# Linear attention and a squared-ReLU MLP on one core: tile 0 loaded on two queues, measured in halves, its products put between its transposes

## The chip, the cores and the metric

The kernel runs on one core of a Trainium2 chip. The core has a matrix engine (TensorE, PE in the profile, with its weight loads shown apart as PEld), three engines for elementwise work (VectorE = DVE, ScalarE = ACT, GpSimd = POOL), SyncE (SP), which issues most loads and stores, and 16 DMA engines. The engines run side by side, each through its own queue in order, and wait for one another on semaphores. The metric is the time of the whole program on the device, in microseconds (us); lower is better.

## What is computed

A layer-normalised input goes through a linear attention with 32 heads of 16 columns and, beside it, through an MLP with a squared ReLU; both results are added to the input.

```python
# x: 2048 x 512, wqkv: 512 x 1536, wo: 512 x 512, w1: 512 x 1376, w2: 1376 x 512, all float32
xn = _layernorm(x, axis=-1)
return x + _A_ref(xn, A_wqkv, A_wo) + _B_ref(xn, B_w1, B_b1, B_w2, B_b2)
# _A_ref
q, k, v = qkv[0], qkv[1], qkv[2]                       # of x @ wqkv, by heads
phi = lambda t: jnp.where(t > 0, t + 1, jnp.exp(t)) + 1e-6
pq, pk = phi(q), phi(k)
kv = jnp.einsum("bhsd,bhse->bhde", pk, v)
z = jnp.einsum("bhsd->bhd", pk)
num = jnp.einsum("bhqd,bhde->bhqe", pq, kv)
den = jnp.einsum("bhqd,bhd->bhq", pq, z)[..., None] + 1e-6
return (num / den, heads side by side) @ wo
# _B_ref
h = xn @ w1 + b1;  r = jnp.where(h > 0, h, 0);  return (r * r) @ w2 + b2
```

## The kernel before

The 2048 rows are 16 tiles of 128 tokens. Every product in float32 is made from parts: an operand is split into a high part (a rounded copy, type fp32r) and a low part (what the rounding left), and three products, high by high, high by low and low by high, are summed in PSUM.

The work runs in stages. First, for each tile: load, mean and variance, normalisation, transposition, the projection to the keys (`pk`), phi, and the sum over the tokens of keys by tokens (`kx`). Then come small matrices per head, and after them two large passes over the tokens with queries, both MLP matrices and the output. Nothing schedules the instructions: each engine runs them in the order of the program's text (`manual_schedule`), which was written out by hand. Only the waits are put in by the framework.

The change touches the start, tiles 0 and 1 and the key weights. What happens there, by names:

- 11 matmuls on zeros (`warm`, L528) keep TensorE busy until data is there.
- `touch` (L77, L78) is a tiny load of 64 elements of `wqkv` that ScalarE issues first of all, followed by the load of its function table.
- `load_x(i, t)` (L159) has SyncE load a tile's 128 x 512 values into `xr[i]`. Behind tiles 0 and 1 stand the four chunks of the key weights (`rk`), then tiles 2 and 3.
- `measure` (L232) runs `bn_stats` and `bn_aggr` on VectorE: mean and variance in `mv`. `roots` (L244) adds 1e-5 on VectorE (for tiles 2 and 3 on GpSimd) and has GpSimd raise that to the power -0.5, into `y`.
- VectorE normalises tile 0 in two halves of 256 columns (L600) and tile 1 whole (L270), into `xp`.
- `turned_pe` (L305) has TensorE transpose the four 128 x 128 blocks of `xp[i]` into PSUM (`pt`), and then `ones(i)` (L346) has GpSimd overwrite the last column of `xp[i]` with 1. `transposed` (L314) gives back `high`, ScalarE's copy of the transposed blocks to `xs1h`, `low`, VectorE's rest in `xs1l`, and `keep_t`.
- `heads_k(j)` (L577) is ScalarE's high part of key chunk j (`wkh`), `rests_k(eng, j)` (L581) the low part (`wkl`), on GpSimd ("pool") or VectorE ("dve").
- `some(i, u, js)` (L587) are the products of tile i's chunks js (part u) with the high key part, `rest(j, i)` (L590) those of its high part with the low key part. A projection is finished by 12 such products.
- GpSimd's small copy at L611 orders the load of tiles 4 to 7 behind tile 1's normalisation.

In the order of the text, between the measuring of tiles 0 and 1 and `rest(0, 0)`:

```python
    high, low, keep0 = transposed(0, 2)
    heads_k(0)
    high()
    rests_k("pool", 0)
    some(0, 0, (0,), True)
    normalise(*two_tiles[1])
    high1, low1, keep1 = transposed(1, 2)
    heads_k(1)
```

Of the kernel before, what the change touches and what calls it, by code (L numbers as in the profile page):

```python
# [18 lines left out]
def kernel(  # L19
# [55 lines left out]
    ctx.enter_context(tc.manual_schedule())  # L75

    touch = keep.tile([D // Q * 4, 1], F32, name="touch")  # L77
    nc.scalar.dma_start(touch, wqkv.rearrange("(a b) c -> a b c", b=Q // 4)[:, 0, D:D + 1])  # L78
    nc.scalar.preload_act_table_set("natural_log_exp_and_others")

# [224 lines left out]
    def turned_pe(i, n=1):  # L305

        t = [bank(f"pt{i}{k}", "acc" if i < 2 else "ps")[:, :D // n] for k in range(n)]
        for j in range(NJ):
            k, at = divmod(j * P, D // n)
            nc.tensor.transpose(t[k][:, at:at + P], xp[i][:, j * P:(j + 1) * P], ident)  # L310
        ones(i)
        return [p.rearrange("p (j t) -> p j t", j=NJ // n) for p in t]

    def transposed(i, n=1):  # L314

        b, at = i // TB, slot(i)
        if i < NDVE:
            t = turned_pe(i, n)
# [12 lines left out]
        def keep_t():  # L331
# [5 lines left out]
            if i < NPE:  # L337
                nc.sync.dma_start(xTd[b][:, :, at], o)

        return high, low, keep_t  # L340

# [187 lines left out]
    t, rk = two("x0"), four("rk", "r0")  # L529
    for i in range(2):  # L530
        load_x(i, t[:, i:i + 1])
    def load_k(*js):
# [61 lines left out]
    two_tiles = group(0), group(1)  # L594
    for t in two_tiles:
        measure(t)
        roots(*t)
    for k in range(2):
        a = slice(k * D // 2, (k + 1) * D // 2)
        nc.vector.tensor_scalar(xp[0][:, a], xr[0][:, a], two_tiles[0][2][:, 0, 0:1], two_tiles[0][3][:, 0, :1],  # L600
                                op0=OP.subtract, op1=OP.mult)
    high, low, keep0 = transposed(0, 2)
    heads_k(0)
    high()
    rests_k("pool", 0)
    some(0, 0, (0,), True)
    normalise(*two_tiles[1])
# [3 lines left out]
    nc.gpsimd.tensor_copy(x4[:, 0, :1], xp[1][:, :1])  # L611
    load_x(4, x4)
    some(0, 0, (1,))
    low()
    some(0, 1, (0, 1))
    high(1)
# [10 lines left out]
    heads_k(2)  # L627
    rests_k("dve", 1)
    high1(1)
# [773 lines left out]
```

## Time and profile before

| | |
|---|---|
| median of 3 runs | 409.11 us (408.92 to 409.43) |
| profiled execution | 409.03 us, its span 407.3 us |
| TensorE busy | 402.2 us, 99% |
| VectorE busy | 308.0 us, 76% |
| ScalarE busy | 268.4 us, 66% |
| GpSimd busy | 49.7 us, 12% |
| moved by DMA | 49.00 MB, 120 GB/s in the mean |

The profile is of one execution. Its time is the span, from the first instruction to the last, and 1.7 us around it. A line of the timeline gives the start in us from the span's start, the length, the engine, the line of the kernel, the operation, what it writes and reads and its shape; `x4` means that four like it stand together, and the square bracket gives the idle time of the engine ahead of it and what ended that. Buffers go by the program's names, without their numbers.

### The profile page before, as it was taken

The page shows a single profiled execution, that of the slowest core. Times are in us where ns is not written, and L with a number is a line of the kernel's source. Part 1 is how long each engine was busy: PE and PEld are TensorE (multiplying, and loading weights), DVE is VectorE, ACT ScalarE, POOL GpSimd, SP SyncE. Part 2 cuts the span into 40 slices and gives each one's busy share as a digit, 9 for nine tenths or more (in the row PEclk, how much of TensorE's full clock was granted, in tenths as well). Part 3 has the DMA queues.
Part 4 walks back from the last instruction along what each step waited for, and adds up shares of the span by engine and source line. Part 5 has one row for each costly group of instructions (what it writes and reads, how often), then busy time and mean ns, then how long its engine had stood idle before and what let it go on. Part 6 is the DMA issues. An engine that isn't in the chain of part 4 may idle for free.

```text
span 407.3 us, 5632 instructions
## 1 busy us (share of the span) xinstructions
PE 402.2 (99%) x1939; PEld 331.0 (81%) x1939; DVE 308.0 (76%) x559; ACT 268.4 (66%) x466; POOL 49.7 (12%) x81
## 2 busy tenths in 40 slices
PE   8999999999999999999999999999999999999996
PEld 7888888888788888888878888888888888878885
DVE  5886666587898989988349997667989676449833
ACT  5677677556887788886818752667687856828520
POOL 5444333220000000030000300000000200001200
PEclk9999999999999999999999999999999999999999
DMA  6857646900432231380564903311222880034612
GB/s 212 278 175 224 208 163 192 256 27 0 120 90 80 77 103 27 121 200 16 217 228 146 194 19 113 106 53 52 52 80 50 226 189 26 0 108 151 105 26 103
DMA packets 46830, 49.00 MB, mean 120 GB/s; under 512 B 8337, under 2 KB 31121, under 8 KB 46546
## 3 DMA queue, kind: packets, MB, share of 16 engines
q1 hardware_dynamic: 44418, 44.46, 35.4%
q0 software_dynamic: 2304, 4.20, 6.5%
q8 instruction: 15, 0.25, 0.2%
q14 instruction: 13, 0.11, 0.1%
q10 hardware_dynamic: 80, 0.00, 0.0%
HBM read 37.76 MB, written 9.70 MB: 117 GB/s over the span
## 4 chain that ended last, share of the span: by engine, by line
PE 98%; DMA 1%; DVE 1%; ACT 0%; issue 0%
PE acc L133 37%; PE b L497 33%; PE pk L378 11%; PE kx L398 11%; PE acc L508 2%; PE pz L133 1%; DMA x<-in_A_x_dram 1%; PE b L133 1%; PE pz0b L133 1%; PE acc L515 0%; PE pt L310 0%; DVE st L236 0%; PE pkv L937 0%; PE pm L954 0%; PE end L133 0%; PE end L508 0%
## 5 line engine op out<-in xcount | busy, mean ns | idle before, releaser
L133 PE MATMUL acc<-w2r,s 128*128 128x512 f32 x477 | 112.8, 390 | 0.0
L133 PEld LDWEIGHTS acc<-w2r,s 128*128 128x128 f32 x477 | 89.4, 188 | 19.3 <-issue 0.7
L497 PE MATMUL b<-T,aop 128*128 128x512 f32 x336 | 83.5, 389 | 0.0
L497 PEld LDWEIGHTS b<-T,aop 128*128 128x128 f32 x336 | 63.0, 188 | 13.9 <-ACT t L114 0.8
L1075 POOL DMA_DIRECT2D res<-in_B_b_dram x16 | 14.4, 1067 | 276.7 <-DVE pt L438 90.4
L398 PE MATMUL kx<-pk,tok 128*128 128x512 f32 x192 | 46.0, 389 | 0.0
L398 PEld LDWEIGHTS kx<-pk,tok 128*128 128x128 f32 x192 | 36.0, 188 | 7.6 <-ACT pk L114 0.2
L497 PE MATMUL b<-xs0h,aop 128*128 128x512 f32 x112 | 36.9, 390 | 0.0
L133 PE MATMUL acc<-mh,aTsr 128*128 128x512 f32 x112 | 35.6, 389 | 0.0
L1083 DVE TENSOR_TENSOR res<-acc,res 128x512 f32<-128x512 f32 x16 | 10.7, 689 | 20.5 <-PE acc L133 19.2
L114 ACT ACTIVATE aop<-S 128x512 fp32r<-128x512 f32 x28 | 17.5, 624 | 12.5 <-DVE S L735 12.5
L359 POOL TENSOR_TENSOR tok<-xp,tok 128x512 fp32r<-128x512 f32 x15 | 20.2, 1344 | 39.6 <-ACT tok L114 39.6
L497 PEld LDWEIGHTS b<-xs0h,aop 128*128 128x128 f32 x112 | 21.0, 188 | 4.4
L133 PEld LDWEIGHTS acc<-mh,aTsr 128*128 128x128 f32 x112 | 21.0, 188 | 4.4
L125 DVE TENSOR_TENSOR w2r<-r,w2r 128x512 fp32r<-128x512 f32 (+2 forms) x35 | 23.8, 682 | 0.5 <-ACT w2r L114 0.4
L122 DVE TENSOR_TENSOR aop<-S,aop 128x512 fp32r<-128x512 f32 x28 | 19.3, 688 | 4.8 <-ACT aop L114 4.4
L122 DVE TENSOR_TENSOR s<-c,s 128x512 fp32r<-128x512 f32 x20 | 13.6, 689 | 11.4 <-ACT s L114 11.3
L497 PE MATMUL b<-xs0l,aop 128*128 128x512 f32 x56 | 21.8, 389 | 0.0
L133 PE MATMUL acc<-ml,aTsr 128*128 128x512 f32 x56 | 21.8, 389 | 0.0
L114 ACT ACTIVATE w2r<-r 128x512 fp32r<-128x512 f32 x32 | 19.6, 619 | 3.3 <-DMA out_dram<-res 2.0
L497 PE MATMUL b<-xs1h,aop 128*128 128x512 f32 x56 | 19.5, 389 | 0.0
L114 ACT ACTIVATE T<-Tf 128x512 fp32r<-128x512 f32 x16 | 9.5, 624 | 14.4 <-DVE Tf L678 14.3
(195 smaller groups left out, 751.6 us busy)
## 6 DMA issues: line engine op xcount, KB each, us to landing
r<-in_B_w_dram SPq DMA_DIRECT2D x49, 256.0 KB, 3.2
res<-in_A_x_dram SPq DMA_DIRECT2D x8, 512.0 KB, 4.2
res<-in_B_b_dram POOLq DMA_DIRECT2D x16, 256.0 KB, 5.7
out_dram<-res SPq DMA_DIRECT2D x15, 256.0 KB, 2.1
via<-xp SPq DMA_DIRECT2D x5, 512.0 KB, 2.6
xg<-via SPq DMA_DIRECT2D x20, 128.0 KB, 2.8
xTd<-t SPq DMA_DIRECT2D x8, 256.0 KB, 3.4
x<-in_A_x_dram SPq DMA_DIRECT2D x4, 512.0 KB, 4.1
```

Of the source, the lines that this page charges most:

```text
L114: nc.scalar.activation(o, i, AF.Copy, bias=bias)
L122: ENG[el].tensor_tensor(out=l, in0=src, in1=f32(h), op=OP.subtract)
L125: nc.vector.tensor_tensor(out=l, in0=src, in1=f32(h), op=OP.subtract)
L133: nc.tensor.matmul(ps, lhsT=a[u], rhs=b[v], start=first and n == 0, stop=last and n == 2)
L359: ENG[el].tensor_tensor(out=l, in0=src, in1=f32(h), op=OP.subtract)
L378: nc.tensor.matmul(ps, lhsT=cols(i)[u][:, j, slot(i)], rhs=w[v][:, j, :], start=first and n == 0, stop=last and n == len(steps) - 1)
L398: nc.tensor.matmul(kxp[c], lhsT=tok[i][:, u, c * P:(c + 1) * P], rhs=pk[i][:, v], start=i == 0 and (u, v) == first, stop=i == NT - 1 and ( ...
L497: nc.tensor.matmul(ps, lhsT=a[u][:, j * P:(j + 1) * P], rhs=b[v][:, j, :], start=first and j == 0 and n == 0, stop=last and j == 1 and n == 2,
L508: nc.tensor.matmul(ps, lhsT=s[u][:, k * P:(k + 1) * P], rhs=w2s[NF - 1][u][:, a:z], start=first and u == 0, stop=stop and u == 1)
L1075: nc.gpsimd.dma_start(r[:, i], b2[None, :].partition_broadcast(P), accum_op=OP.add)
L1083: nc.vector.tensor_tensor(out=r[:, a:z], in0=ps, in1=r[:, a:z], op=OP.add)
```

## The change

1. Tile 0 is loaded in two halves of 256 columns, the left one by SyncE's queue and the right one by ScalarE's, ahead of `touch` and the table load. Tile 1 stays on SyncE's queue.
2. `bn_stats` of tile 0 runs on each half, and `bn_aggr` joins the two. VectorE's order is then: tile 1's `bn_stats`, tile 0's left half normalised, tile 1's `bn_aggr` and addition, tile 0's right half normalised.
3. `turned_pe` no longer issues the transposes itself but gives back `part(k)`, and `transposed` takes a function `between` that it calls after the first part. For tile 0 that is the first key chunk's high part, the left half's high part and the first product.
4. The left half's low part and its product come ahead of tile 1.
5. The low part of key chunk 1 is made on GpSimd, behind the copy of L611, instead of on VectorE.

```diff
-    touch = keep.tile([D // Q * 4, 1], F32, name="touch")
-    nc.scalar.dma_start(touch, wqkv.rearrange("(a b) c -> a b c", b=Q // 4)[:, 0, D:D + 1])
-    nc.scalar.preload_act_table_set("natural_log_exp_and_others")
...
     def turned_pe(i, n=1):
         t = [bank(f"pt{i}{k}", "acc" if i < 2 else "ps")[:, :D // n] for k in range(n)]
-        for j in range(NJ):
-            k, at = divmod(j * P, D // n)
-            nc.tensor.transpose(t[k][:, at:at + P], xp[i][:, j * P:(j + 1) * P], ident)
-        ones(i)
-        return [p.rearrange("p (j t) -> p j t", j=NJ // n) for p in t]
-
-    def transposed(i, n=1):
+
+        def part(k):
+            for at in range(0, D // n, P):
+                nc.tensor.transpose(t[k][:, at:at + P], xp[i][:, k * D // n + at:][:, :P], ident)
+            if k == n - 1:
+                ones(i)
+
+        return [p.rearrange("p (j t) -> p j t", j=NJ // n) for p in t], part
+
+    def transposed(i, n=1, between=None):
...
+        if i < NDVE:
+            for k in range(n):
+                part(k)
+                if between and k == 0:
+                    between(high, low)
         return high, low, keep_t
...
     t, rk = two("x0"), four("rk", "r0")
-    for i in range(2):
-        load_x(i, t[:, i:i + 1])
+    touch = keep.tile([D // Q * 4, 1], F32, name="touch")
+    left, right = slice(0, D // 2), slice(D // 2, D)
+    xr[0] = t[:, 0]
+    nc.sync.dma_start(xr[0][:, left], xf[:P, left])
+    nc.scalar.dma_start(xr[0][:, right], xf[:P, right])
+    nc.scalar.dma_start(touch, wqkv.rearrange("(a b) c -> a b c", b=Q // 4)[:, 0, D:D + 1])
+    nc.scalar.preload_act_table_set("natural_log_exp_and_others")
+    load_x(1, t[:, 1:])
...
     two_tiles = group(0), group(1)
-    for t in two_tiles:
-        measure(t)
-        roots(*t)
-    for k in range(2):
-        a = slice(k * D // 2, (k + 1) * D // 2)
-        nc.vector.tensor_scalar(xp[0][:, a], xr[0][:, a], two_tiles[0][2][:, 0, 0:1], two_tiles[0][3][:, 0, :1],
-                                op0=OP.subtract, op1=OP.mult)
-    high, low, keep0 = transposed(0, 2)
-    heads_k(0)
-    high()
+    _, st, mv, y = two_tiles[0]
+    for k, a in enumerate((left, right)):
+        nc.vector.bn_stats(st[:, k, :], xr[0][:, a])
+    nc.vector.bn_aggr(mv[:, 0, :], st[:, :2, :])
+    roots(*two_tiles[0])
+
+    def half(a):
+        nc.vector.tensor_scalar(xp[0][:, a], xr[0][:, a], mv[:, 0, 0:1], y[:, 0, :1], op0=OP.subtract, op1=OP.mult)
+
+    nc.vector.bn_stats(two_tiles[1][1][:, 0, :], xr[1])
+    half(left)
+    nc.vector.bn_aggr(two_tiles[1][2][:, 0, :], two_tiles[1][1][:, 0, :])
+    roots(*two_tiles[1])
+    half(right)
+
+    def between(high, low):
+        heads_k(0)
+        high()
+        some(0, 0, (0,), True)
+
+    high, low, keep0 = transposed(0, 2, between)
     rests_k("pool", 0)
-    some(0, 0, (0,), True)
+    low()
+    some(0, 1, (0,))
     normalise(*two_tiles[1])
     high1, low1, keep1 = transposed(1, 2)
     heads_k(1)
     nc.gpsimd.tensor_copy(x4[:, 0, :1], xp[1][:, :1])
     load_x(4, x4)
+    rests_k("pool", 1)
     some(0, 0, (1,))
-    low()
-    some(0, 1, (0, 1))
+    some(0, 1, (1,))
...
-    rests_k("dve", 1)
```

TensorE's queue at the start, before: `pt_159` and `pt_160` are the two halves of tile 0, `pt_171` and `pt_172` those of tile 1, `pk_140` is tile 0's projection.

```order
L528 MATMUL warm<-const-float32-0.0 128x128 x11
L310 MATMUL pt_159<-ident,xp_80 128x128 x2
L310 MATMUL pt_160<-ident,xp_80 128x128 x2
L378 MATMUL pk_140<-wkh,xs1h 128x512
L310 MATMUL pt_171<-ident,xp_80 128x128 x2
L310 MATMUL pt_172<-ident,xp_80 128x128 x2
L378 MATMUL pk_140<-wkh,xs1h 128x512
L378 MATMUL pk_140<-wkh,xs1l 128x512 x2
L378 MATMUL pk_140<-wkl,xs1h 128x512
```

TensorE's queue at the same place in the changed kernel, where the halves of tile 0 are `pt_161` and `pt_162`, those of tile 1 `pt_175` and `pt_176`, and tile 0's projection is `pk_141`.

```order
L532 MATMUL warm<-const-float32-0.0 128x128 x11
L307 MATMUL pt_161<-ident,xp_77 128x128 x2
L382 MATMUL pk_141<-wkh,xs1h 128x512
L307 MATMUL pt_162<-ident,xp_77 128x128 x2
L382 MATMUL pk_141<-wkh,xs1l 128x512
L307 MATMUL pt_175<-ident,xp_77 128x128 x2
L307 MATMUL pt_176<-ident,xp_77 128x128 x2
L382 MATMUL pk_141<-wkh,xs1h 128x512
L382 MATMUL pk_141<-wkh,xs1l 128x512
L382 MATMUL pk_141<-wkl,xs1h 128x512
```

The first product now stands between tile 0's halves, the second between tile 0 and tile 1; four products stand ahead of the first one with the low key part (`wkl`), as before.

GpSimd's queue from the two powers on, before: the `MEMSET`s are `ones(0)` and `ones(1)`, `wkl` is the low part of key chunk 0, and `y_197` belongs to tile 2.

```order
L248 TENSOR_TENSOR y_145<-y_145,power 128x1
L248 TENSOR_TENSOR y_148<-y_148,power 128x1
L348 MEMSET xp_80 128x1
L583 TENSOR_TENSOR wkl<-rk,wkh 128x512
L348 MEMSET xp_80 128x1
L611 COPY x_134<-xp_80 128x1
L247 TENSOR_SCALAR y_197<-mv_196 128x1
L248 TENSOR_TENSOR y_197<-y_197,power 128x1
```

GpSimd's queue in the changed kernel, where the second `wkl` is that of key chunk 1 and `y_200` belongs to tile 2.

```order
L244 TENSOR_TENSOR y_146<-y_146,power 128x1
L244 TENSOR_TENSOR y_149<-y_149,power 128x1
L352 MEMSET xp_77 128x1
L593 TENSOR_TENSOR wkl<-rk,wkh 128x512
L352 MEMSET xp_77 128x1
L633 COPY x_135<-xp_77 128x1
L593 TENSOR_TENSOR wkl<-rk,wkh 128x512
L243 TENSOR_SCALAR y_200<-mv_199 128x1
L244 TENSOR_TENSOR y_200<-y_200,power 128x1
```

The order up to the first `wkl` is the same; its memset still stands behind all of tile 0's transposes. The second `wkl` is new ahead of tile 2's steps.

VectorE's queue at the start, before: `x_112` holds tiles 0 and 1, the third and sixth rows are the additions of 1e-5 for tiles 0 and 1.

```order
L236 BN_STATS st_143<-x_112 128x6
L237 BN_AGGR mv_144<-st_143 128x2
L247 TENSOR_SCALAR y_145<-mv_144 128x1
L236 BN_STATS st_146<-x_112 128x6
L237 BN_AGGR mv_147<-st_146 128x2
L247 TENSOR_SCALAR y_148<-mv_147 128x1
L600 TENSOR_SCALAR xp_80<-x_112,mv_144,y_145 128x256 x2
L270 TENSOR_SCALAR xp_80<-x_112,mv_147,y_148 128x512
L329 TENSOR_TENSOR xs1l<-pt_159,xs1h 128x2x128
L329 TENSOR_TENSOR xs1l<-pt_160,xs1h 128x2x128
```

VectorE's queue in the changed kernel, with the same roles for `x_109`, `y_146` and `y_149`.

```order
L607 BN_STATS st_144<-x_109 128x6 x2
L608 BN_AGGR mv_145<-st_144 128x2
L243 TENSOR_SCALAR y_146<-mv_145 128x1
L614 BN_STATS st_147<-x_109 128x6
L612 TENSOR_SCALAR xp_77<-x_109,mv_145,y_146 128x256
L616 BN_AGGR mv_148<-st_147 128x2
L243 TENSOR_SCALAR y_149<-mv_148 128x1
L612 TENSOR_SCALAR xp_77<-x_109,mv_145,y_146 128x256
L328 TENSOR_TENSOR xs1l<-pt_161,xs1h 128x2x128
L266 TENSOR_SCALAR xp_77<-x_109,mv_148,y_149 128x512
L328 TENSOR_TENSOR xs1l<-pt_162,xs1h 128x2x128
```

Tile 0's left half now stands ahead of tile 1's `bn_aggr` and addition, and its low part (`xs1l`) ahead of tile 1's normalisation.

More of the change, by code (lines that the diff above doesn't have):

```diff
@@ L307, in turned_pe @@
         t = [bank(f"pt{i}{k}", "acc" if i < 2 else "ps")[:, :D // n] for k in range(n)]
-        for j in range(NJ):
-            k, at = divmod(j * P, D // n)
-            nc.tensor.transpose(t[k][:, at:at + P], xp[i][:, j * P:(j + 1) * P], ident)
-        ones(i)
-        return [p.rearrange("p (j t) -> p j t", j=NJ // n) for p in t]
-    def transposed(i, n=1):
+        def part(k):
[5 more added lines that the diff above has]
+    def transposed(i, n=1, between=None):
         b, at = i // TB, slot(i)
         if i < NDVE:
-            t = turned_pe(i, n)
+            t, part = turned_pe(i, n)
         else:
```

## The prediction

> **What bounds the kernel now.** I read the page first, for the engine that is always busy and for its clock.
>
> ```profile
> span 407.3 us, 5632 instructions
> PE 402.2 (99%) x1939; PEld 331.0 (81%) x1939; DVE 308.0 (76%) x559; ACT 268.4 (66%) x466; POOL 49.7 (12%) x81
> PEclk9999999999999999999999999999999999999999
> PE 98%; DMA 1%; DVE 1%; ACT 0%; issue 0%
> ```
>
> TensorE is busy for 99% of the span, and the chain that ended last is 98% TensorE. So the change can act only through the moment at which TensorE's unbroken run begins, or through holes that it opens in that run. The chain in order of time (start, length, what) and the list of all that TensorE waited for show where the run begins:
>
> ```profile
> 0.79 2.85 DMA x<-in_A_x_dram
> ...
> 3.66 0.70 DVE st L236
> ...
> 6.14 0.45 PE pt L310 x2
> ...
> 7.99 4.38 PE pk L378 x19
> ...
> 12.81 3.71 PE pk L378 x16
> 16.51 5.47 PE kx L398 x24
> 21.98 2.72 PE pk L378 x12
> ```
> ```profile
> PE pt L310 <- DVE xp L600: 0.7, 1, 0.7
> ```
>
> The load of tile 0 lands at 0.79 + 2.85 = 3.64. From 7.99 on TensorE works without a hole: 19 products in 4.38 us, 0.23 us each, and 12 in 2.72 later. Apart from its start its only listed wait is the 0.7 us for tile 0's normalised half. What the change is worth is therefore read in the first 13 us, and a shift there is carried to the end whole. The timeline of that stretch (start, length, engine, line, operation; idle time before it and its releaser in brackets) carries the terms below:
>
> ```profile
> 0.83 4.57 PE L528 MATMUL warm<-const-float32-0.0 128*128 128x128 f32 x22 [0.83 <-PEq L1389]
> ...
> 4.61 0.15 DVE L247 TENSOR_SCALAR y<-mv 128x1 f32<-128x1 f32 x1
> ...
> 4.92 0.57 POOL L248 TENSOR_TENSOR y<-y,power 128x1 f32<-128x1 f32 x1 [1.76 <-DVE y L247]
> 5.24 0.63 ACT L114 ACTIVATE wkh<-rk 128x512 fp32r<-128x512 f32 x1 [2.58 <-DMA rk<-in_A_wqkv_dram]
> ...
> 5.61 0.15 DVE L247 TENSOR_SCALAR y<-mv 128x1 f32<-128x1 f32 x1
> 5.68 0.73 DVE L600 TENSOR_SCALAR xp<-x,mv,y 128x256 f32<-128x256 f32 x2
> ...
> 6.14 0.76 PE L310 MATMUL pt<-ident,xp 128*128 128x128 f32 x4 [0.74 <-DVE xp L600]
> 6.54 0.55 DVE L270 TENSOR_SCALAR xp<-x,mv,y 128x512 f32<-128x512 f32 x1
> 6.62 0.39 ACT L326 ACTIVATE xs1h<-pt 128x256 fp32r<-128x256 f32 x1 [0.75 <-PE pt L310]
> ...
> 6.97 0.16 POOL L348 MEMSET xp<- 128x1 f32 x1 [0.46 <-PE pt L310]
> ...
> 7.05 0.50 PE L378 MATMUL pk<-wkh,xs1h 128*128 128x512 f32 x1
> 7.06 1.30 POOL L583 TENSOR_TENSOR wkl<-rk,wkh 128x512 fp32r<-128x512 f32 x1
> ...
> 7.39 0.60 PE L310 MATMUL pt<-ident,xp 128*128 128x128 f32 x4
> ...
> 7.83 0.82 DVE L329 TENSOR_TENSOR xs1l<-pt,xs1h 128x256 fp32r<-128x256 f32 x2 [0.37 <-ACT xs1h L326]
> ...
> 8.41 0.19 PEld L378 LDWEIGHTS pk<-wkl,xs1h 128*128 128x128 f32 x1 [0.16 <-POOL xp L348]
> 8.53 0.39 PE L378 MATMUL pk<-wkl,xs1h 128*128 128x512 f32 x1
> ...
> 8.67 0.70 DVE L236 BATCH_NORM_STATS2 st<-x 128x6 f32<-128x512 f32 x1
> ...
> 9.50 0.66 DVE L583 TENSOR_TENSOR wkl<-rk,wkh 128x512 fp32r<-128x512 f32 x1
> 9.68 0.58 POOL L247 TENSOR_SCALAR y<-mv 128x1 f32<-128x1 f32 x1 [1.16 <-DVE mv L237]
> 10.34 0.57 POOL L248 TENSOR_TENSOR y<-y,power 128x1 f32<-128x1 f32 x1
> ...
> 11.23 0.52 DVE L270 TENSOR_SCALAR xp<-x,mv,y 128x512 f32<-128x512 f32 x1
> ...
> 12.21 0.60 PE L310 MATMUL pt<-ident,xp 128*128 128x128 f32 x4
> ```
>
> Two things stand out. VectorE starts tile 0's first half only at 5.68, although GpSimd's power is done at 4.92 + 0.57 = 5.49, because tile 1's statistics (last small step at 5.61) are queued ahead of it. And GpSimd's low part of the first key chunk ends at 7.06 + 1.30 = 8.36, just before TensorE asks for it at 8.41: that product is the fifth of the projection, and it has no slack to give.
>
> **The change part by part.** *The load.* Both halves together are the same bytes as before. The halves' landing is not in the trace; the nearest rows are those of DMAs by size (KB each, median us to landing), and the traffic at that time (busy time of each engine, clock, DMA share, GB/s).
>
> ```profile
> r<-in_B_w_dram SPq DMA_DIRECT2D x49, 256.0 KB, 3.2
> ...
> r<-in_B_w_dram SPq DMA_DIRECT2D x5, 128.0 KB, 2.6
> ...
> touch<-in_A_wqkv_dram ACTq DMA_DIRECT2D x1, 0.2 KB, 3.0
> ```
> ```profile
> 3.00:4.00 1.00, 1.00 (x7) 1.00 (x7) 0.34 (x1) 0.00 (x0) 0.16 (x1) 1.00 1.06 365
> ```
>
> Early bound: 128 KB lands 0.6 us sooner than 256 KB, so 3.64 - 0.6 = 3.04. Late bound: ScalarE's own queue landed even 0.2 KB only at 0.79 + 3.0 = 3.79, and 128 KB at 365 GB/s are 0.36 us, together 4.15. I take 3.64 for the later half, between the two: the same bytes through engines that are fully used (share 1.06) should end at the same time; and the left half at least 0.35 us sooner. The Trainium skill, "DMA: Bandwidth & Descriptors", section "Issuing engines are not separate DMA queues", speaks against a gain here: DMAs from several engines share the same 16 DMA engines, and only the issue time is saved. No run here shows yet whether it holds for this pair; by it the sum stands as taken, and by the early bound it would be 0.4 us better.
>
> *The statistics.* Rows by shape, with mean ns, give what halving the width does on VectorE:
>
> ```profile
> L329 DVE TENSOR_TENSOR xs1l<-pt,xs1h 128x256 fp32r<-128x256 f32 x4 | 1.7, 423 | 0.4 <-ACT xs1h L326 0.4
> ...
> L329 DVE TENSOR_TENSOR xs1l<-pt,xs1h 128x512 fp32r<-128x512 f32 x1 | 0.7, 693 | 0.1
> ```
>
> So after the right half lands I expect 0.42 us instead of 0.69 (between 0.35, half, and 0.69, no gain): the small step that was at 4.61 comes at 4.34. GpSimd starts 0.31 us after that (4.92 - 4.61) and takes 0.57, to 5.22; with 0.05 for the signal VectorE's left half starts at 5.27 instead of 5.68, a gain of 0.41. Tile 1's statistics pass, now ahead of it, runs from 4.41 to 5.10 and is hidden under GpSimd's power, as long as tile 1 has landed by 4.6. Before, its last small step at 5.61 with a pass of 0.70 ahead puts that landing at 4.9 at the latest; at 4.9 the left half would come at 5.6 and 0.33 of the gain would be lost. Transposes follow 0.46 later (6.14 - 5.68), at 5.73; the warm-up ends at 0.83 + 4.57 = 5.40 and doesn't bind. ScalarE's copy follows 0.48 after that (6.62 - 6.14), at 6.21, clear of its key-chunk copy (5.24 to 5.87), and the first product 0.43 later, at 6.64 instead of 7.05. Up to here it is 0.41 us faster.
>
> *The order.* The right half's two transposes now stand behind that product. Behind it the next TensorE step can start after 0.23 us (the pitch above) to 0.34 (7.05 to 7.39): 6.87. Two transposes take 0.38 to the end of the last (0.11 of pitch, from four in 0.60, and 0.27): 7.25, where before tile 0's transposes ended at 6.14 + 0.76 = 6.90. GpSimd's queue waits for just this: its memset of the last column overwrites what the transposes read, and the low part of chunk 0 stands behind it. Before it started 0.16 after the end of the transposes (7.06 - 6.90); so now at 7.41, ends at 8.71, and the product that needs it starts 0.17 later (8.53 - 8.36), at 8.88. Four products are done ahead of it in both orders, so this is a loss of 0.35 us for everything behind. With the upper bounds (0.34 and 0.45 for the transposes' start and length, the last from the chain's 6.14 row) it is 0.53. I take 0.45.
>
> TensorE alone would not be late: tile 1's normalisation on VectorE now stands behind the low part of tile 0's left half, so 6.60 + 0.03 + 0.40 (pitch of 7.83's two) = 7.03, plus 0.55 makes 7.58; tile 1's transposes follow at 7.63, and the fifth product could start at 8.5, as before. The hole that opens, 0.35 to 0.5 us, is GpSimd's. The Trainium skill, "SBUF — State Buffer", section "Who interferes with whom", says that GpSimd and certain VectorE steps lock each other out of a shared port for a whole instruction. The rows of 6.54 and 7.06 overlap by 0.03 us, which is within what GpSimd's spans can show; by the rule the low part could not start before 7.58, and the loss would be 0.52, inside the bounds above.
>
> *The second low part.* VectorE loses 0.66 us at 9.50; GpSimd gains 1.30 ahead of tile 2's small steps. Its chunk 0 ends at 8.8, chunk 1 with the memset and the small copy before it at 9.0 to 10.3; TensorE needs it about nine products after the fifth, at 11.0. Tile 2's two steps follow to 11.5 (0.58 and 0.57), its normalisation ends at 12.1, and its transposes stand at 12.21 + 0.45 = 12.66. So it is covered by 0.5 us; without the cover it would cost the rest. The freed VectorE time is on no wait that ends last.
>
> *What else moves.* The touch and the table load start one DMA issue later; the first key chunk is wanted by ScalarE at 5.24 and could come 0.3 us later without harm. The load of tile 2 is now issued only when the right half has landed, and is read at 8.67, 5 us after that. All cost nothing.
>
> Sum: the profiled execution took 409.03 us, of which 407.3 are the span and 1.73 lie around it. 409.03 + 0.45 = 409.48, and from the median of the runs, 409.11, it is 409.56. I predict **409.5 us**.
>
> **The rivals.** *A, the forecast*: TensorE's fifth product waits for GpSimd; +0.2 to +0.7 us with a landing between 3.5 and 3.8. For it: the row 8.41 and its releaser. Chance 0.53.
>
> *B, the halves land early* (3.04 to 3.4): the left half would be normalised at 4.7, then the warm-up's end and the key-chunk copy at 5.87 bind; the first product comes at about 6.2, the fifth at 8.43 instead of 8.53. That is -0.1 to +0.1 us, 409.0 to 409.2. For it are the 128 KB rows, against it the full DMA engines. Chance 0.22.
>
> *C, slower: ScalarE's queue lands late*. The measuring of tile 0 ends with the later of two queues; at 4.15 all of the above is 0.51 later, +1.0 us, 410.1. It turns from A where the landing passes about 4.0. For it is the touch row, against it that this tiny DMA shared its engines with tile 0's load. Chance 0.19.
>
> *D, the clock*: the warm-up's pitch of 4.57 / 22 = 0.21 us against 0.11 for the same shape in 7.39's row shows a half-speed TensorE at first. More idle time between 5.4 and 9 us could bring that back: 4 us of work at half speed lose some 2 us, 411. The Trainium skill, "TensorE: Matmul & The Clock Gate", Part 1, gives about 3.4 us of idling for that; no hole here would be longer than 0.8 us. Against it also: before had 0.74 us idle at the same place and no drop shows in its clock row. Chance 0.03.
>
> *E, a gain from something that the rows don't show*: 0.03.
>
> **How the numbers follow.** A measurement of this kernel tells about 0.2%, 0.8 us, from no change. The range takes A and B whole and C up to its price, with the 0.1 us by which runs lie off their median: 409.0 to 410.2. Only D and E lie outside, and the tails of A and C. Faster by over 0.2% needs E: 0.04 with a little of B. Slower by over 0.2% needs D or most of C: 0.19. The rest, 0.77, is within 0.2%.
>
> **What would show it.** In the profile after: tile 0's statistics step at 4.3; the first product at about 6.6; chunk 0's low part on GpSimd starting at 7.4 and not before the last transpose of tile 0; a TensorE hole of 0.3 to 0.5 us with GpSimd as its releaser ahead of the first product with the low key part; tile 2's transposes at 12.6. I am wrong if GpSimd starts that low part at 7.06 or sooner, if the hole is not there, or if the right half lands outside 3.5 to 3.8.

## The result, and the profile after

| | before | after |
|---|---|---|
| median of 13 runs each, side by side | 409.09 us (408.59 to 411.27) | 410.14 us (409.73 to 411.41) |
| ratio after / before, 95% interval | | 1.0024 [1.0013, 1.0036] |
| profiled execution | 409.03 us, span 407.3 | 410.27 us, span 408.6 |

The change makes the kernel 1.05 us slower. The bound of 0.2% lies inside the interval. In the one execution of the kernel after above 411 us TensorE's clock dropped for a while (granted clock 0.996 over the whole span); the last section comes back to this, and it doesn't set the median.

The page of the kernel after: TensorE is as busy as before, 403.3 us instead of 402.2, and the chain that ended last is TensorE's for 97%.

```profile
span 408.6 us, 5635 instructions
PE 403.3 (99%) x1939; PEld 331.5 (81%) x1939; DVE 307.4 (75%) x559; ACT 268.2 (66%) x466; POOL 50.1 (12%) x82
PE 97%; issue 1%; DMA 1%; DVE 1%; POOL 0%; POOLq 0%
```

The list of what TensorE waited for in the kernel after (us in total, times, longest) has two entries that before did not have, one for ScalarE's copy of tile 0's left half, one for GpSimd:

```profile
PE pk L382 <- ACT xs1h L325: 0.9, 1, 0.9
...
PE pk L382 <- POOL xp L352: 0.2, 1, 0.2
```

The chain that ended last, in order of time, shows that TensorE's unbroken run begins at 9.48 with the fifth product (before has no hole from its first product, at 7.05, on, and its fifth is at 8.53), and that the first big step behind the projection of tile 1 (`kx`) comes at 17.59 instead of 16.51:

```profile
0.79 2.42 DMA x<-in_A_x_dram
...
9.48 3.93 PE pk L382 x16
...
17.59 5.45 PE kx L402 x24
```

These 1.08 us, of the 1.24 between the two profiled executions, are carried to the end. The timeline of the first 10 us of the kernel after has where they arise:

```profile
0.83 5.03 PE L532 MATMUL warm<-const-float32-0.0 128*128 128x128 f32 x22 [0.83 <-PEq L1410]
...
3.23 0.75 DVE L607 BATCH_NORM_STATS2 st<-x 128x6 f32<-128x256 f32 x2 [3.23 <-DMA x<-in_A_x_dram]
...
5.18 0.41 DVE L612 TENSOR_SCALAR xp<-x,mv,y 128x256 f32<-128x256 f32 x1 [0.16 <-POOL y L244]
5.66 0.68 PE L307 MATMUL pt<-ident,xp 128*128 128x128 f32 x2
6.30 0.63 ACT L110 ACTIVATE wkh<-rk 128x512 fp32r<-128x512 f32 x1 [3.23 <-DMA rk<-in_A_wqkv_dram]
6.83 0.37 ACT L325 ACTIVATE xs1h<-pt 128x256 fp32r<-128x256 f32 x1
7.25 0.51 PE L382 MATMUL pk<-wkh,xs1h 128*128 128x512 f32 x1 [0.92 <-ACT xs1h L325]
7.57 0.54 DVE L266 TENSOR_SCALAR xp<-x,mv,y 128x512 f32<-128x512 f32 x1
7.60 0.38 PE L307 MATMUL pt<-ident,xp 128*128 128x128 f32 x2
8.04 0.11 POOL L352 MEMSET xp<- 128x1 f32 x1 [1.42 <-PE pt L307]
8.13 1.29 POOL L593 TENSOR_TENSOR wkl<-rk,wkh 128x512 fp32r<-128x512 f32 x1
...
8.17 0.66 PE L307 MATMUL pt<-ident,xp 128*128 128x128 f32 x4
...
8.89 0.40 PE L382 MATMUL pk<-wkh,xs1l 128*128 128x512 f32 x1
...
9.48 0.50 PE L382 MATMUL pk<-wkl,xs1h 128*128 128x512 f32 x1 [0.18 <-POOL xp L352]
```

Read it in two pieces. Up to tile 0's first transposes everything is early: 5.66 instead of 6.14. Then ScalarE gets the first key chunk only at 6.30 (before: 5.24), its copy of the left half is queued behind that, and the first product starts at 7.25, 0.20 later than before's 7.05. In the second piece, from the first product to the fifth (the first one with `wkl`), 2.23 us pass (7.25 to 9.48), where before needed 1.48 (7.05 to 8.53): the 0.75 us between them are the chain right half's transposes (7.60 to 7.98), memset (8.04), low part (8.13 to 9.42), product (9.48). 0.20 and 0.75 make the 0.95 by which the fifth product is late.

Not all of the 0.75 is GpSimd's. The product ahead of the fifth starts at 8.89, and products follow one another every 0.23 us, so TensorE alone would have reached the fifth at about 9.12, 1.87 us behind the first. That is 0.39 more than the 1.48 of before, because tile 1's normalisation stands behind the left half's low part now and tile 1's transposes come only at 8.17. GpSimd's chain, which runs beside this one and ends later, adds 0.36.

The DMA issues of the first 10 us (count, KB each, median us to landing): the halves landed sooner than tile 0's 256 KB did (2.85 in before), and only 0.2 us apart.

```profile
x<-in_A_x_dram ACTq DMA_DIRECT2D x1, 128.0 KB, 2.6
x<-in_A_x_dram SPq DMA_DIRECT2D x1, 128.0 KB, 2.4
touch<-in_A_wqkv_dram ACTq DMA_DIRECT2D x1, 0.2 KB, 3.7
```

### The profile page after: what moved, and what is told of

Its sections match the earlier page's. It is cut to its first block, busy times and chain, and to the rows that moved or that the text cites. A ratio compares the mean times of both kernels' runs of the same rounds, so it can differ in the third digit from the quotient of the medians.

```text
span 408.6 us, 5635 instructions
## 1 busy us (share of the span) xinstructions
PE 403.3 (99%) x1939; PEld 331.5 (81%) x1939; DVE 307.4 (75%) x559; ACT 268.2 (66%) x466; POOL 50.1 (12%) x82
## 4 chain that ended last, share of the span: by engine, by line
PE 97%; issue 1%; DMA 1%; DVE 1%; POOL 0%; POOLq 0%
PE acc L129 37%; PE b L501 33%; PE kx L402 11%; PE pk L382 11%; PE acc L512 2%; PE pz L129 1%; PE b L129 1%; PE pz0b L129 1%; DMA x<-in_A_x_dram 1%; PE acc L519 0%; PE pkv L958 0%; PE pm L975 0%; POOL y L244 0%; DVE st L607 0%; PE end L129 0%
## 5 line engine op out<-in xcount | busy, mean ns | idle before, releaser
L1104 DVE TENSOR_TENSOR res<-acc,res 128x512 f32<-128x512 f32 x16 | 10.7, 689 | 20.7 <-PE acc L129 19.3
```

Source lines behind the costliest of these rows:

```text
L1104: nc.vector.tensor_tensor(out=r[:, a:z], in0=ps, in1=r[:, a:z], op=OP.add)
```

## The experiments

The table has, for each kernel, the median, the median of before in the same job, the ratio with its interval, and from its profile's timeline: the start of tile 0's first statistics (tile 0 is there), of ScalarE's high part of key chunk 0, of the first product, of the fifth, and the time between these two. All times in us.

| kernel | median (runs) | before | ratio | tile 0 | chunk 0 | first | fifth | between |
|---|---|---|---|---|---|---|---|---|
| before | 409.09 (13) | | | 3.66 | 5.24 | 7.05 | 8.53 | 1.48 |
| after | 410.14 (13) | 409.09 | 1.0024 [1.0013, 1.0036] | 3.23 | 6.30 | 7.25 | 9.48 | 2.23 |
| e1 touch first | 412.49 (6) | 409.10 | 1.0080 [1.0067, 1.0094] | 5.84 | 6.00 | 8.96 | 11.85 | 2.89 |
| e2 no touch | 409.41 (11) | 409.10 | 1.0005 [0.9996, 1.0013] | 3.52 | 5.01 | 7.14 | 8.61 | 1.47 |
| e3 memset behind | 410.24 (10) | 409.10 | 1.0030 [1.0021, 1.0039] | 3.68 | 5.14 | 7.01 | 9.64 | 2.63 |
| e4 both | 412.90 (6) | 409.10 | 1.0096 [1.0080, 1.0112] | 5.08 | 5.71 | 8.09 | 11.35 | 3.26 |
| e5 after again | 411.37 (1) | | | 3.25 | 6.45 | 7.40 | 10.56 | 3.16 |
| e6 load only | 409.56 (11) | 409.13 | 1.0009 [1.0001, 1.0018] | 3.52 | 5.43 | 6.84 | 8.73 | 1.89 |
| e7 order only | 409.70 (11) | 409.13 | 1.0008 [0.9994, 1.0021] | 3.31 | 5.14 | 6.70 | 8.92 | 2.22 |
| e8 normalise first | 411.69 (6) | 409.13 | 1.0073 [1.0053, 1.0094] | 3.57 | 5.78 | 7.15 | 10.13 | 2.98 |
| e9 GpSimd only | 409.04 (11) | 408.98 | 1.0000 [0.9992, 1.0009] | 3.68 | 6.02 | 7.07 | 8.54 | 1.47 |
| e10 after, no touch | 410.16 (6) | 408.98 | 1.0032 [1.0020, 1.0043] | 3.66 | 5.63 | 7.22 | 9.43 | 2.21 |
| e11 load, old order | 409.28 (11) | 408.98 | 1.0006 [0.9997, 1.0015] | 3.62 | 5.14 | 7.10 | 8.58 | 1.48 |

For e1 and e4 "tile 0" is the later half. In the profiles of e1, e4 and e5 TensorE's clock was halved for a while ahead of the fifth product. Letters in the expectations name theories. The first four runs set T against O. T: `touch`, now behind the right half on ScalarE's queue, makes the key chunk late, and that is the loss. O: the loss is GpSimd's, whose memset stands behind the last transposes of tile 0.

### e1, after with the touch issued first

```diff
+    nc.scalar.dma_start(touch, ...)
     nc.scalar.dma_start(xr[0][:, right], xf[:P, right])
-    nc.scalar.dma_start(touch, ...)
```

> The changed kernel with one edit: ScalarE issues the small touch of the weights first and tile 0's right half second. Theory T (the touch opens the way for the weight loads, and 0.44 us of delay on it made the first key chunk 1.06 us late): ScalarE's first key chunk starts at 5.2 to 5.4 again instead of 6.30, the first product comes at 6.6 to 6.8 instead of 7.25, the first product with the low key part at 8.8 to 9.0 instead of 9.48, and the time is +0.3 to +0.6 us over before. Rival Q (two queues share the DMA engines and slow the weights, whatever the touch does): the key chunk stays at 6.1 to 6.4 and the time at +0.9 to +1.2 us.

Measured: 412.49, 2.35 above the kernel after. Five of the six executions had a granted clock of 0.996 or less over the span; the sixth took 411.19, 1.05 above the kernel after. T fell: the key chunk came at 6.00, not at 5.24, although the touch was first. What the edit did do was to make the right half late. The timeline and the DMA issues of this kernel:

```profile
3.06 0.43 DVE L607 BATCH_NORM_STATS2 st<-x 128x6 f32<-128x256 f32 x1 [3.06 <-DMA x<-in_A_x_dram]
5.84 0.43 DVE L607 BATCH_NORM_STATS2 st<-x 128x6 f32<-128x256 f32 x1 [2.35 <-DMA x<-in_A_x_dram]
7.93 0.56 PE L307 MATMUL pt<-ident,xp 128*128 128x128 f32 x2 [2.57 <-DVE xp L612]
```
```profile
x<-in_A_x_dram ACTq DMA_DIRECT2D x1, 128.0 KB, 4.4
```

The same 128 KB on the same queue took 2.6 us as that queue's first DMA and 4.4 behind a DMA of 0.2 KB. It was also issued later, at 1.38 instead of 0.79, and so behind the 256 KB of tile 1 (1.24); whether the tiny DMA or that place made it late is not shown. That a half on ScalarE's queue lands late is rival C, which the change itself avoids by issuing the half first.

### e2, before without the touch

```diff
-    nc.scalar.dma_start(touch, ...)
```

> The kernel before without the touch of the weights (64 values that nothing reads). Theory T: without it the first key chunk comes 0.8 us or more later than its 5.24, the first product at 7.25 instead of 7.05, and the time rises by 0.2 to 0.8 us. Rival Q: the chunk stays at 5.1 to 5.3 and the time is the same within 0.1 us.

Measured: 409.41, a difference from before that the interval doesn't tell from none. The first product is at 7.14 and the fifth at 8.61, where before has 7.05 and 8.53. The touch is no help to the key chunk and no harm, so T has nothing left here; e10 takes the touch out of the kernel after.

### e3, after with the memset of tile 0 behind the low part

```diff
-            if k == n - 1:
+            if k == n - 1 and i:
                 ones(i)
...
     rests_k("pool", 0)
+    ones(0)
```

> The changed kernel with one edit: GpSimd makes the first key chunk's low part ahead of its memset of tile 0's last column, so that it no longer waits for tile 0's transposes. Theory O (the order on GpSimd opened the hole ahead of the first product with the low key part): the low part starts when the high part is done, 7.0 instead of 8.13, that product comes at 9.1 instead of 9.48, and the time is +0.6 to +0.8 us over before. Rival P (TensorE's own order makes it late, GpSimd only looked like it): the product stays at 9.4 to 9.5 and the time at +1.0 us.

Measured: 410.24, no better than after. Yet O's mechanism is there, as the timeline shows: with the memset out of the way GpSimd starts the low part at 7.04, before the right half's transposes and not after them. The gain is eaten by VectorE's normalisation of tile 1, which takes 1.30 us instead of 0.54:

```profile
7.04 1.27 POOL L593 TENSOR_TENSOR wkl<-rk,wkh 128x512 fp32r<-128x512 f32 x1
7.33 1.30 DVE L266 TENSOR_SCALAR xp<-x,mv,y 128x512 f32<-128x512 f32 x1
8.69 0.66 PE L307 MATMUL pt<-ident,xp 128*128 128x128 f32 x4 [0.72 <-DVE xp L266]
9.64 0.40 PE L382 MATMUL pk<-wkl,xs1h 128*128 128x512 f32 x1
```

The normalisation is issued at 7.33, within GpSimd's instruction, and ends only behind it; tile 1's transposes then wait 0.72 us. The Trainium skill, "SBUF — State Buffer", section "Who interferes with whom", says that GpSimd and a VectorE step such as `tensor_scalar` in its two-port form exclude each other for a whole instruction, and that the one issued first wins. This trace agrees: the normalisation ends 0.32 us behind the low part, at 8.63 and 8.31, and in e8 below by the same 0.32, at 8.52 and 8.20. So the memset's late place keeps the low part out of the normalisation's way; taking it away trades one wait of TensorE for another. No kernel here shows O without that collision. Nor could O have won back all of the 0.75: TensorE's own order, 1.87 us from the first product to the fifth, would have put the fifth at about 8.88 here, an estimate from the rows of the kernel after.

### e4, e1 and e3 together

```diff
 # e1, and e3
-    nc.scalar.dma_start(touch, ...)          # behind the right half
+    nc.scalar.dma_start(touch, ...)          # ahead of it
     rests_k("pool", 0)
+    ones(0)
```

> The changed kernel with both edits, the touch first and the low part ahead of the memset. If T and O are the two causes, the first product comes at 6.6 to 6.8, the first with the low key part at 8.5 to 8.7, and the time is within 0.2 us of before. If only one of them holds, it is the time of that one alone: +0.4 (T) or +0.7 (O).

Measured: 412.90. The right half came at 5.08, the normalisation of tile 1 took 1.30 us again. Both effects are there at once, and neither edit helps. Five of the six executions had a dropped clock, as in e1.

### e5, the kernel after once more

> The changed kernel once more, unaltered, for a second profile of it. Its first profile had ScalarE's first key chunk at 6.30, while the run with the memset moved, whose loads are the same, had it at 5.14. Theory V (the landing of the first loads changes from execution to execution, and the order alone costs about 1 us): the chunk comes at another time than 6.30 by more than 0.3 us, and the first product with the low key part still at 9.2 to 9.6, 0.7 to 1.0 us later than before. Rival L (late weights are the rule with the right half on ScalarE's queue): 6.1 to 6.5 again.

Measured: one execution of 411.37 us at a clock of 0.996. Tile 0 came at 3.25 and the key chunk at 6.45, as in the first profile of this kernel (3.23 and 6.30). So what L says came again, but L is no rule: with the right half first on ScalarE's queue the chunk came at 5.14 in e3 and, below, at 5.43 (e6), 5.78 (e8), 5.63 (e10) and 5.14 (e11). In addition the clock dropped from 7.30 to 10.7, which is taken up at the end.

### e6 and e7, the two parts of the change by themselves

e6 is the kernel before with the halved load, its statistics and VectorE's new order up to the normalisation of tile 0; TensorE's and GpSimd's order and the rest stay. e7 is the kernel before with the first product between the transposes and the left half's low part ahead of tile 1; load and statistics stay. Both leave key chunk 1's low part on VectorE.

```diff
 # e6
-    for i in range(2):
-        load_x(i, t[:, i:i + 1])
+    nc.sync.dma_start(xr[0][:, left], xf[:P, left])
+    nc.scalar.dma_start(xr[0][:, right], xf[:P, right])
+    load_x(1, t[:, 1:])
 ...
+    nc.vector.bn_stats(two_tiles[1][1][:, 0, :], xr[1])
+    half(left)
+    nc.vector.bn_aggr(two_tiles[1][2][:, 0, :], two_tiles[1][1][:, 0, :])
+    roots(*two_tiles[1])
+    half(right)
 # e7
-    high, low, keep0 = transposed(0, 2)
+    high, low, keep0 = transposed(0, 2, between)
     rests_k("pool", 0)
+    low()
+    some(0, 1, (0,))
```

> The kernel before with the loading and the measuring of the changed one alone: two queues, halves, VectorE's new order, and all of tile 0's transposes together again, ahead of the first product; the second low part back on VectorE. Theory V: the first product with the low key part comes at 8.1 to 8.4 and the time is 0.1 to 0.4 us below before. Rival L: the late weights cost 0.3 to 0.8 us here too.

> The kernel before with the order of the products alone: the first product between tile 0's halves, the low part of the left half ahead of tile 1's normalisation; loads, statistics and the second low part as before. Theory V: the low key part starts on GpSimd at 7.8 to 8.0 instead of 7.06, its product comes at 9.2 to 9.5, and the time is +0.7 to +1.0 us. Rival L: within 0.3 us of before.

Measured: 409.56 for e6, 409.70 for e7, 0.43 and 0.57 above before. e7's interval includes a ratio of 1, and before had three executions of 410 us or more in that job; but the lowest of e7's eleven, 409.57, lies above 19 of before's 23. With e9's 0.06 the three parts add to 1.06 us, near the change's 1.05. This is no proof that the parts are the change's: what costs e6 its time, as shown below, is not found in the kernel after. e7's loss is less than expected (0.7 to 1.0), with GpSimd at 7.58 and the fifth product at 8.92, both sooner than expected. Its timeline has the forecast chain:

```profile
6.70 0.50 PE L386 MATMUL pk<-wkh,xs1h 128*128 128x512 f32 x1 [0.47 <-ACT xs1h L329]
7.48 0.12 POOL L356 MEMSET xp<- 128x1 f32 x1 [1.33 <-PE pt L311]
7.58 1.29 POOL L591 TENSOR_TENSOR wkl<-rk,wkh 128x512 fp32r<-128x512 f32 x1
8.92 0.51 PE L386 MATMUL pk<-wkl,xs1h 128*128 128x512 f32 x1 [0.16 <-POOL xp L356]
```

Tile 0 happened to come at 3.31 in this execution, 0.35 earlier than in before's. Even so the fifth product is 0.39 later; from the first product on it takes 2.22 us, as in the kernel after.

e6 is neither V's gain nor L's loss by late weights: its chunk, at 5.43, was in time for a copy at 6.41. The timeline tells why the fifth product is late, though the first is 0.21 earlier than before's:

```profile
6.24 0.66 POOL L244 TENSOR_TENSOR y<-y,power 128x1 f32<-128x1 f32 x1 [0.81 <-DVE y L243]
6.93 0.55 DVE L266 TENSOR_SCALAR xp<-x,mv,y 128x512 f32<-128x512 f32 x1 [0.46 <-POOL y L244]
7.13 1.50 POOL L585 TENSOR_TENSOR wkl<-rk,wkh 128x512 fp32r<-128x512 f32 x1
7.53 0.66 PE L306 MATMUL pt<-ident,xp 128*128 128x128 f32 x4 [0.20 <-DVE xp L266]
8.73 0.45 PE L374 MATMUL pk<-wkl,xs1h 128*128 128x512 f32 x1
```

With tile 0's left half ahead of tile 1's aggregation, tile 1's power comes later on GpSimd, so its normalisation starts at 6.93 instead of 6.54. It now begins ahead of GpSimd's low part and holds that one up, 1.50 us instead of 1.30: the lock of e3 with the roles exchanged. The low part ends at 8.63, 0.27 later than before's 8.36. That is just covered: TensorE has no idle time from tile 1's transposes on, and these, at 7.53 instead of 7.39, carry the late normalisation to the fifth product. The chain that ended last goes through them and not through GpSimd.

### e8, after with the low part first and tile 1's normalisation ahead of the left half's low part

```diff
 # e3, and
     ones(0)
+    normalise(*two_tiles[1])
     low()
     some(0, 1, (0,))
-    normalise(*two_tiles[1])
```

> The changed kernel with GpSimd's first low key part ahead of the memset, and tile 1's normalisation on VectorE ahead of the low part of tile 0's left half, so that neither the transposes nor the normalisation stand behind the other. Theory K (with only the memset moved, GpSimd's 1.3 us low part kept VectorE's normalisation of tile 1 waiting, 1.30 us instead of 0.54): the normalisation takes 0.55 again, tile 1's transposes start at 7.5 to 7.9, the product with the low part at 8.4 to 8.8, and the time is within 0.3 us of before. Rival: the normalisation is long for another reason and stays at 1.3 us, +0.8 us.

Measured: 411.69. This median lies between three executions of 410.83 to 410.97 and three of 412.41 to 413.64 with a dropped clock (0.996 or less); already the first three are about 0.7 us above the kernel after. K's cause is there, but the edit is no remedy: the normalisation took 1.53 us, not 0.55. In the timeline GpSimd's low part starts 0.06 us ahead of the normalisation and keeps it out all the same, and the left half's low part is then late too:

```profile
6.93 1.27 POOL L593 TENSOR_TENSOR wkl<-rk,wkh 128x512 fp32r<-128x512 f32 x1
6.99 1.53 DVE L266 TENSOR_SCALAR xp<-x,mv,y 128x512 f32<-128x512 f32 x1 [0.46 <-POOL y L244]
8.90 0.50 PE L382 MATMUL pk<-wkh,xs1l 128*128 128x512 f32 x1 [1.03 <-DVE xs1l L328]
```

### e9, before with the second low part on GpSimd

```diff
     load_x(4, x4)
+    rests_k("pool", 1)
...
-    rests_k("dve", 1)
```

> The kernel before with the second key chunk's low part alone moved to GpSimd. Forecast from the cover seen in the profiles (0.3 to 0.5 us ahead of tile 2's normalisation): tile 2's transposes at 12.1 to 12.4 as before (12.21), the time within 0.15 us of before. Rival: its 1.3 us on GpSimd push tile 2's power and normalisation, transposes at 12.5 or later, +0.3 us or more.

Measured: 409.04 against 408.98, ratio 1.0000, with tile 2's transposes at 12.18 (before 12.21): the second low part is covered. Its profile has something else. The key chunk came at 6.02, on the old load with one queue, and the copy of tile 0 was still in time:

```profile
6.02 0.63 ACT L114 ACTIVATE wkh<-rk 128x512 fp32r<-128x512 f32 x1 [3.37 <-DMA rk<-in_A_wqkv_dram]
...
6.63 0.38 ACT L326 ACTIVATE xs1h<-pt 128x256 fp32r<-128x256 f32 x1
7.07 0.50 PE L378 MATMUL pk<-wkh,xs1h 128*128 128x512 f32 x1
```

So a late chunk is not peculiar to the two queues, and here it had just no cost: the copy started 0.47 behind the transposes (6.16), where before has 0.48. In the kernel after and in e5, where the copy did wait for the chunk's, it started 0.53 behind that one (6.30 and 6.83, 6.45 and 6.98). So for a copy at 6.21, as the prediction had it, the chunk must come by 5.68.

### e10, after without the touch

```diff
-    nc.scalar.dma_start(touch, ...)
```

> The changed kernel without the touch of the weights (64 values that nothing reads). With two queues the first key chunk came at 5.14 to 6.45 in seven profiles, with one at 5.01 to 5.24 in three. Theory W (the touch, now behind the right half, falls into the loads and holds the weights up): the chunk comes at 5.0 to 5.3, the first product at 6.6 to 6.9, the time 0.3 to 0.6 us below the changed kernel's 410.1. Rival Z (two queues on the same engines hold them up): still 5.6 or later, the time within 0.2 us of the changed kernel's.

The theories here were W, that the late key chunk is what costs the kernel after its gain, so that it runs faster when the chunk is in time; and Z, that the order sets the time whichever of the two loads is early. Measured: 410.16, as the kernel after. The timeline:

```profile
3.66 0.75 DVE L606 BATCH_NORM_STATS2 st<-x 128x6 f32<-128x256 f32 x2 [3.66 <-DMA x<-in_A_x_dram]
5.63 0.63 ACT L110 ACTIVATE wkh<-rk 128x512 fp32r<-128x512 f32 x1 [3.12 <-DMA rk<-in_A_wqkv_dram]
6.07 0.67 PE L307 MATMUL pt<-ident,xp 128*128 128x128 f32 x2 [0.21 <-DVE xp L611]
7.22 0.50 PE L382 MATMUL pk<-wkh,xs1h 128*128 128x512 f32 x1 [0.47 <-ACT xs1h L325]
9.43 0.50 PE L382 MATMUL pk<-wkl,xs1h 128*128 128x512 f32 x1 [0.17 <-POOL xp L352]
```

The chunk was in time, and the first product is at 7.22 nevertheless: now tile 0 came at 3.66, as in before, and the two transposes took 0.67 us, where e6's took 0.44. W fell as the only reason. Z held: 2.21 us from the first product to the fifth, and the same time in the end.

### e11, e6 with VectorE's old order

```diff
     nc.vector.bn_stats(two_tiles[1][1][:, 0, :], xr[1])
-    half(left)
     nc.vector.bn_aggr(two_tiles[1][2][:, 0, :], two_tiles[1][1][:, 0, :])
     roots(*two_tiles[1])
+    half(left)
     half(right)
```

> The run with the loading and measuring alone, with VectorE's old order: tile 1's aggregate and addition ahead of tile 0's halves. Theory Y (with the new order GpSimd gets tile 1's power 0.4 us later, tile 1's normalisation came at 6.93 instead of 6.54, and that ate what the halves brought): the normalisation at 6.3 to 6.6, tile 1's transposes at 7.1 to 7.4, the time 0.2 to 0.5 us below that run's 409.56, so 409.1 to 409.35. Rival: late weights cost it, whatever VectorE's order; 409.5 to 409.7.

Theory Y was that e6's loss comes from VectorE's new order and not from the two queues. Measured: 409.28, not to be told from before. The normalisation of tile 1 is back at 6.59, and the fifth product at 8.58: in the profile Y held. In time it is not shown. e11 is 0.28 below e6, but in another job; each against before in its own job they are 0.30 and 0.43 above it, and the intervals overlap. The run also says that the halved load and statistics, put into the old order, bring nothing that can be measured. None of the eleven is faster than the kernel before.

## Why the prediction was right, and where a step failed

The direction, the place and the mechanism were right. The time lies in the range, but 0.64 us above the 409.5 forecast, because one term of the sum did not arrive. That 410.14 is in the range is partly luck: the range reached to 410.2 for the price of C, and C did not happen.

*The order: right in its mechanism.* From the first product to the fifth the prediction had 2.24 us (6.64 to 8.88); the kernel after has 2.23, e10 2.21, e7 2.22. That it agrees so well is luck, since two errors cancel. The right half's transposes began 0.35 behind the product (0.34 in e10 and e7), at the upper bound and not at the 0.23 of the sum. And the fifth product began 0.06 behind the end of the low part (0.06 in e10, 0.05 in e7), not 0.17: that was read from before, where the fifth product has no idle time ahead of it and so did not wait for GpSimd. GpSimd's start 0.16 after the last transposes became 0.15 (7.98 to 8.13), its length 1.29. Tile 1's normalisation also ended just ahead of that start, at 8.11; but in e6 the low part starts while that normalisation runs and is only longer for it, so the start is the memset's. e3 shows that without the memset GpSimd does start earlier. What the prediction did not see is that this would not help: the memset hid a collision with tile 1's normalisation.

That "TensorE alone would not be late" held only together with the gain of the load. The prediction's 7.58 was the end of tile 1's normalisation, and 7.57 is where it started; it ended at 8.11, as the copy ahead of it all was 0.62 late. Counted from the first product the forecast for TensorE's own order was good, 1.86 us (8.5 - 6.64) and 1.87 measured, but that is 0.39 more than before's 1.48. GpSimd's own addition of 0.36 lies in the forecast 0.35 to 0.5; the profile shows only 0.18 us of it as idle time, as the product ahead (0.40 long, at a pitch of 0.23) fills the rest.

*The load: the failed step.* The 0.41 us by which the first product was to come sooner never came; it was 0.20 later in the kernel after. The term needed the left half to land at least 0.35 us ahead of the right one, so that only one statistics step of 0.42 us would follow the last landing. In all seven profiles in which ScalarE issued the right half first, the halves landed 0.1 to 0.2 us apart, and the two steps took 0.75 us from the first landing on, where the whole tile's one step took 0.69. From the start of the statistics to the first product before needs 3.39 us; e3 and e6, with the chunk in time and transposes of 0.44, need 3.33 and 3.32, e11 with VectorE's old order 3.48. So the new order of VectorE brings about 0.15 us, the halves take some 0.08 of it back, and the term is 0.06 or 0.07 instead of 0.41.

That the transposes still came at 5.66 in the kernel after, where 5.73 was forecast, is luck: tile 0 was there at 3.23, 0.43 sooner than in before (the right half at about 3.4, 0.79 + 2.6, outside the 3.5 to 3.8 of the prediction). In e10, with 3.66, they came at 6.07. Then two things took that gain and 0.20 more. First, the prediction put down that the key chunk "could come 0.3 us later without harm"; it came 1.06 later. Had ScalarE been free when the transposes ended at 6.34, its copy would have stood at about 6.37 and not at 6.83: 0.46 us. Second, the two transposes took 0.68 us instead of 0.44: 0.24 us. Without both the first product would have been at 7.25 - 0.46 - 0.24 = 6.55, near the 6.64 forecast, with the early landing in it. This last sum is argued from one profile, not shown by a run. The sum after that step: instead of -0.41 + 0.76 it is +0.20 + 0.75.

*A cost at nothing that isn't.* VectorE's new order was costed as a pure gain. By itself it delays tile 1's normalisation by 0.39 us (e6, 6.93 instead of 6.54) and with it the fifth product; what that costs in time is not clear of the noise (e6 and e11). In the kernel after it lies under the left half's low part, which the normalisation waits for anyway.

*The second low part: right.* It costs nothing (e9).

*The rivals.* The time is that of C (410.1), but not by C: both halves landed in time. A right half that lands late is seen only with the touch ahead of it (e1, e4). B's early landing is there in both profiles of the kernel after (3.23 and 3.25), but its consequence is not, since it needed the key chunk in time as well. D does not set the median, but does occur.

*Open.* Why the first loads scatter. Over all profiles tile 0 comes between 3.23 and 3.68 (e1 and e4 aside) and the key chunk between 5.01 and 6.45; both profiles with the halves at 3.23 to 3.25 have the chunk at 6.30 and 6.45, while e10 has 3.66 and 5.63. That early halves make a late chunk fits these few; e7 (3.31 and 5.14) speaks against it for one queue. It was not settled. The split into 0.57 and 0.43 is of medians; which steps the runs without a profile took is not known. So it is open how much of the median's 1.05 us is the order, and how much late chunks and slow transposes.

## What to carry to other kernels

Before an operand's part is pulled forward, follow every queue that it doesn't move past: here one product came between the transposes, and a one-column memset on GpSimd that waited for the last transpose carried the delay to TensorE. A gain on one input of a matmul is worth only the smaller of the gains on all its inputs, so bound the other operand's arrival over several executions and not by one profile. Halving a load helps the step behind it only if one half really lands sooner; here they came 0.1 to 0.2 us apart, and two steps on halves took longer than one on the whole. And where GpSimd and VectorE both have half-microsecond steps, fix which goes first: a wait that looks wasteful may keep them apart.

## What the runs showed of the hardware

*The clock drops after a window that is not idle.* The windows of e5, cut where its matmul lengths change (us, busy time and count by engine, granted clock, DMA share, GB/s):

```profile
core 0: us, PE busy (x) PEld busy (x) DVE busy (x) ACT busy (x) POOL busy (x), PEclk, DMA share, GB/s
4.00:7.30 3.30, 1.42 (x11) 0.99 (x10) 1.94 (x8) 0.85 (x3) 1.24 (x2) 1.00 0.94 338
7.30:10.70 3.40, 3.30 (x11) 2.75 (x12) 2.07 (x5) 2.13 (x7) 2.01 (x5) 0.50 0.29 111
10.70:14.00 3.30, 3.30 (x16) 2.70 (x15) 3.16 (x8) 1.61 (x5) 2.42 (x5) 1.00 0.63 215
```

The clock was halved for 3.4 us and came back at once. Ahead of it TensorE had been busy for 1.42 of 3.30 us, with no idle time longer than 1.3. In e1, with 0.83 busy of 3.40, the half-speed stretch is 8.1 to 11.5, as long but at another place. In e5 a product took 0.78 us within the stretch and 0.39 outside, and the execution was 1.2 us longer than the median of its kernel. The Trainium skill, "TensorE: Matmul & The Clock Gate", Part 1, gives a window of 3413 ns that runs freely and isn't tied to the kernel's start, and a drop after an idle window of that length. The length and the changing place agree with these rows; "idle" does not, since the clock dropped behind a window with 1.42 us of work. The prediction's argument against D, that no hole here is near 3.4 us, was thus the wrong one. The rows fit a rule by the sum of the holes in a window better than one by the longest hole; how much work a window needs is not shown. Where there is more idle time at the start such executions are more frequent (granted clock of 0.996 or less over the span in 5 of e1's 6 runs, in 1 of the kernel after's 13).

*A slow start that the granted clock doesn't show.* The 22 matmuls of the warm-up took 4.15 us (e5) to 5.04 (e2) over the profiles, while the clock's column reads 1.00 from the start. Where they took 5.03 and the two transposes followed within 0.21 us (the kernel after, e8, e10), these took 0.67 to 0.69 us; where they took 4.15 to 4.78 (e3, e5, e6, e7), 0.44. That the transposes still ran at the warm-up's slow pace is read from these lengths, not shown by the clock.

*A load issued behind a tiny DMA on its queue landed late:* 4.4 us instead of 2.6 to the landing of 128 KB (e1; 3.7 in e4). Its issue was then also behind that of tile 1, and the two are not told apart.

*The exclusion between GpSimd and VectorE works both ways, and a lead of 0.06 us was enough (e8):* 0.54 became 1.30 (e3) and 1.53 (e8) on VectorE, 1.30 became 1.50 on GpSimd (e6).
